# Attention with a memory, then a mixture of experts: one pass for the last keys' two parts, and a new table for the planner

## The chip, the cores and the metric

The kernel runs on one core of a Trainium2 chip. Five engines work side by side, each through its own queue in order: TensorE (PE: matmuls, and PEld, its weight loads), VectorE (DVE), ScalarE (ACT), GpSimd (POOL) and SyncE (SP, which here only issues transfers). The metric is the time of one execution in microseconds (us).

## The reference

Four batches of 8 heads, 576 tokens each, 64 numbers per head. Each head's output mixes causal softmax attention with a read of a stored memory matrix. The heads of a token are laid side by side as a row of 512; a gate then sends each of the 2304 rows to one of 8 experts, two matrix products with a ReLU between.

```python
scores = scale * np.matmul(q, k.transpose(0, 1, 3, 2))
scores = np.where(causal, -1000000000.0, scores)
a = np.exp(scores - scores.max(-1, keepdims=True))
local = np.matmul(a / (a.sum(-1, keepdims=True) + 1e-09), v)
mem_out = np.einsum('bhsd,bhde->bhse', q_p, M_prev) / mem_norm
attn = g * mem_out + (1 - g) * local
logits = x @ w_gate + modality_bias[modality_id]     # x: attn as 2304 x 512
out[mask] = gate_w[mask, None] * (np.maximum(x[mask] @ w1[e], 0.0) @ w2[e])
```

## The kernel before

**Precision.** Most matrix products take a high part (a rounded copy, fp32r) and a low part (the rest) of an operand, and add products of both. ACT makes the high part from PSUM, DVE subtracts it and leaves the low one.

**A head** (32 of them, two to a pair) goes through stages: `scores` (L657, 12 matmuls; DVE masks them and takes row minima, L669; ACT makes the exponentials, L675), `ptrans` (L684, 15 transposes, which ACT and DVE turn into `pth` and `ptl`, the high and low probabilities with keys on the partitions, L701 and L703), and `av` (L715 and L720: values times `pth`, then values times `ptl`, into two PSUM tiles). 576 keys are five blocks, the fifth of 64 keys only. In that block `pth` and `ptl` still have 128 partitions; the value tile `vhl` holds zeros in the lower 64 rows. Per pair come `prep_q`, `prep_k`, `prep_v`, `memory` and `combine`, and SP's transfers: natural-layout loads (L512, L515, L516) and copies that stack high and low parts (L568, L569).

**A batch** ends with `gate` (rows to DRAM by SP, L808 and L809, and the logits), `route` (expert of each token: small DVE steps, two groups of tiny matmuls, five scatters of token numbers by POOL into three tables, L920) and `rank` (which expert is largest, DVE L932 to L945). After the first batch the weights of the largest expert are streamed in (`load_w`: SP L978, ACT high part L985, DVE or POOL low part L989).

**Expert groups.** A group u is `fetch` (SP reads token numbers, L1009; DVE merges them, L999 and L1000; POOL gathers rows, L1016) and `slot`: transposes L1042, ACT and DVE parts L1050 and L1052, 8 tiles of 12 matmuls each (L1064; ACT L1073, DVE L1075), then per 128 tokens 24 matmuls (L1086) and a store (ACT L1093, POOL L1024). Groups 0 to 2 (one per early batch, 256 tokens) are planned into the attention; group 3 is the first that needs the tables of the last batch. `swap` frees the attention's memory for the second expert.

**Order.** Nothing is issued as written. `Plan` collects operations with an engine, an estimated duration and a priority, and plays them forward: of the operations that could start within `WINDOW[engine]` ns of the earliest, it takes the one of least priority. A priority is a step number plus an offset from `EARLIER`, by stage and engine. The result is a fixed order on each engine; on the chip an instruction waits for its inputs, and all behind it on its engine wait too.

```python
o.prio = at + self.EARLIER.get((stage, eng), 0.0)
lim = first[0] + self.WINDOW[e]
```

## Time and profile before

| what | us |
|---|---|
| median of three runs (lowest, highest) | 553.35 (551.58, 555.19) |
| the profiled execution | 550.81 |
| its span, first to last instruction | 549.1 |
| PE busy in the span | 497.9 |
| DVE, ACT, POOL busy | 330.5, 329.0, 251.9 |

A busy engine is one with an instruction on record; matmul records overlap, so a matmul's rate is read from the distance of two starts, not from its length. A bracket at a row's end is idle time just before the instruction, with what ended it. The granted clock of TensorE has two levels here, 1.00 (2.4 GHz) and 0.50 (1.2 GHz).

### The profile page before, as it was taken

To read this page: it belongs to the slowest core of one execution; us is meant where nothing else is said; L and a number is where in the kernel's file an instruction comes from. 1 tells how busy PE (TensorE), PEld (TensorE's weight loads), DVE (VectorE), ACT (ScalarE), POOL (GpSimd) and SP (SyncE) were. 2 spreads that over 40 slices of the span, in tenths; PEclk is the share of its full clock that TensorE was granted. 3 is DMA by queue.
4 is the path that set the end of the run, shared out by engine and by line. 5 is a ranking of instruction groups with operands and counts; after the bars stand their busy time and mean duration, and the time that the engine had idled before them with its cause. 6 is when DMAs were issued, how large, how long until landed. Compare 5 with 4: busy or idle time off the path is not lost. (4 is left out here: it accounts for less than half of the span.)

```text
span 549.1 us, 10861 instructions
## 1 busy us (share of the span) xinstructions
PE 497.9 (91%) x3420; PEld 445.1 (81%) x3420; DVE 330.5 (60%) x1066; ACT 329.0 (60%) x923; POOL 251.9 (46%) x257
## 2 busy tenths in 40 slices
PE   8898899987899889979898999769999999999992
PEld 8787888875787778869897898769897987989891
DVE  3788788897798988988878336653315512313010
ACT  4798898986999979979298244333325513222110
POOL 8462984656788768865761062350030004010100
PEclk9799899999899989989899999979999999999997
DMA  5888887988777997953740025474036203000100
GB/s 96 189 206 169 206 201 182 231 189 154 192 176 198 238 189 191 220 164 95 180 110 3 20 61 180 78 233 146 18 96 182 83 19 88 29 19 21 40 0 36
DMA packets 97101, 70.43 MB, mean 128 GB/s; under 512 B 73936, under 2 KB 74320, under 8 KB 97042
## 3 DMA queue, kind: packets, MB, share of 16 engines
q1 hardware_dynamic: 93330, 59.99, 45.2%
q0 software_dynamic: 3712, 9.72, 5.8%
q8 instruction: 28, 0.46, 0.4%
q14 instruction: 31, 0.25, 0.2%
HBM read 32.36 MB, written 10.16 MB: 77 GB/s over the span
## 5 line engine op out<-in xcount | busy, mean ns | idle before, releaser
L675 ACT ACTIVATE P<-P,nm 128x576 f32<-128x576 f32 (+4 forms) x160 | 88.5, 558 | 9.1 <-DVE nm L669 6.0
L1024 POOL DMA_INDIRECT out_dram<-osb,ids x19 | 18.9, 997 | 156.0 <-ACT osb L1093 115.3
L1064 PE MATMUL pa<-xh,w1h 128*128 128x256 f32 (+2 forms) x288 | 84.4, 293 | 2.6 <-ACT xh L1050 2.6
L1064 PE MATMUL pa<-xl,w1h 128*128 128x256 f32 (+2 forms) x288 | 83.4, 290 | 0.5 <-DVE xl L1052 0.3
L1064 PE MATMUL pa<-xh,w1l 128*128 128x256 f32 (+2 forms) x288 | 83.1, 288 | 0.0
L1075 DVE SCALAR_TENSOR_TENSOR hlo<-pa,hh 128x256 fp32r<-128x256 f32 (+1 forms) x72 | 29.8, 416 | 69.8 <-ACT hh L1073 69.7
L703 DVE TENSOR_TENSOR ptl<-pa,pth 128x512 fp32r<-128x512 f32 (+1 forms) x128 | 65.6, 564 | 3.0 <-ACT pth L701 2.4
L1073 ACT ACTIVATE hh<-pa 128x256 fp32r<-128x256 f32 (+1 forms) x80 | 29.0, 367 | 61.1 <-PE pa L1064 54.2
L669 DVE CUSTOM_DVE_ANT_0 P<-pa,maskw 128x320 f32<-128x320 f32 (+3 forms) x160 | 62.2, 427 | 4.2 <-PE pa L657 3.5
L684 PE MATMUL pa<-ident,P 128*128 128x128 f32 x320 | 57.6, 285 | 4.0 <-ACT P L675 3.7
L657 PE MATMUL pa<-ks,qs 128*128 128x192 f32 (+3 forms) x186 | 55.5, 329 | 5.9 <-ACT avt L735 2.9
L1086 PE MATMUL pa<-w2h,hh 128*128 128x512 f32 (+1 forms) x152 | 60.4, 397 | 0.0
L701 ACT ACTIVATE pth<-pa 128x512 fp32r<-128x512 f32 (+1 forms) x128 | 57.0, 511 | 5.0 <-PE pa L684 4.4
L1086 PE MATMUL pa<-w2l,hh 128*128 128x512 f32 (+1 forms) x152 | 59.6, 392 | 0.0
L1064 PEld LDWEIGHTS pa<-xh,w1h 128*128 128x128 f32 x288 | 55.6, 193 | 3.4 <-ACT xh L1050 2.9
L1064 PEld LDWEIGHTS pa<-xl,w1h 128*128 128x128 f32 x288 | 55.6, 193 | 1.2 <-DVE xl L1052 0.9
L1086 PE MATMUL pa<-w2h,hlo 128*128 128x512 f32 (+1 forms) x144 | 56.5, 392 | 0.0
L1064 PEld LDWEIGHTS pa<-xh,w1l 128*128 128x128 f32 x288 | 55.5, 193 | 0.0
L1093 ACT ACTIVATE osb<-pa,ids 128x512 f32<-128x512 f32 (+1 forms) x19 | 13.1, 687 | 68.4 <-PE pa L1086 63.1
L657 PE MATMUL pa<-kls,qs 128*128 128x192 f32 (+3 forms) x186 | 49.2, 295 | 0.4 <-DMA kls<-kl 0.4
L684 PEld LDWEIGHTS pa<-ident,P 128*128 128x128 f32 x320 | 40.4, 147 | 6.3 <-ACT P L675 6.0
L684 PE MATMUL pa<-swp,P 128*128 128x128 f32 x160 | 39.5, 287 | 6.1 <-DVE kl L617 2.5
(234 smaller groups left out, 1198.9 us busy)
## 6 DMA issues: line engine op xcount, KB each, us to landing
ks<-kh SPq DMA_DIRECT2D x62, 144.0 KB, 3.0
kls<-kl SPq DMA_DIRECT2D x62, 144.0 KB, 3.4
raw<-in_moe_w_dram SPq DMA_DIRECT2D x32, 256.0 KB, 3.5
qn<-in_q_dram SPq DMA_DIRECT2D x32, 144.0 KB, 4.3
kn<-in_k_dram SPq DMA_DIRECT2D x32, 144.0 KB, 4.2
qs<-qh SPq DMA_DIRECT2D x31, 144.0 KB, 2.6
qs<-ql SPq DMA_DIRECT2D x31, 144.0 KB, 2.7
vn<-in_v_dram SPq DMA_DIRECT2D x32, 128.0 KB, 3.0
```

Source lines behind the costliest of these rows:

```text
L657: nc.tensor.matmul(t.ap[0:m, o:o + z - x], lhsT=l[:, QS[j]:QE[j]], rhs=r[:, x:z], start=(i == 0), stop=(i == len(terms) - 1))
L669: nc.vector.tensor_tensor_reduce(out=pj[:, x:z], in0=t.ap[0:m, o:o + z - x], in1=mk, scale=-1.0, scalar=nm if x else 3.0e38, op0=ALU.add, ...
L675: g.op("ACT", act_ns(w, False, 2), lambda pj=pj, nm=nm, den=den, w=w: nc.scalar.activation(out=pj[:, 0:w], in_=pj[:, 0:w], func=AF.Exp, sc ...
L684: nc.tensor.transpose(t[:, o:o + P], prow[c % NPB][j][:, kb * P:(kb + 1) * P], swp if j == kb else ident)
L701: g.op("ACT", act_ns(n), lambda t=t, o=o, n=n: nc.scalar.activation(out=hi[:, o:o + n], in_=t.ap[:, 0:n], func=AF.Copy), r=[t], w=[("ph_", ...
L703: g.op("DVE", dve_ns(n), lambda t=t, o=o, n=n: nc.vector.tensor_tensor(out=lo[:, o:o + n], in0=t.ap[:, 0:n], in1=hi[:, o:o + n].bitcast(F3 ...
L1024: g.op("POOL", 1310, lambda: nc.gpsimd.indirect_dma_start(out=out[:, :], out_offset=bass.IndirectOffsetOnAxis(ap=ids[u % 4][0:m, t, 0:1].b ...
L1064: nc.tensor.matmul(hp.ap[:, 0:n_], lhsT=a[:, c, f * P:(f + 1) * P], rhs=x_[:, c, 0:n_], start=(n == 0), stop=(n == 3 * KC - 1))
L1073: g.op("ACT", act_ns(z - a), lambda f=f, hp=hp, i=i, a=a, z=z: nc.scalar.activation(out=hh[i][:, f, 0:z - a], in_=hp.ap[:, a:z], func=AF.R ...
L1075: g.op("DVE", dve_ns(z - a), lambda f=f, hp=hp, i=i, a=a, z=z: nc.vector.scalar_tensor_tensor(out=hlo[i][:, f, 0:z - a], in0=hp.ap[:, a:z] ...
L1086: nc.tensor.matmul(op.ap[0:m], lhsT=a[:, f, ts], rhs=w_[:, f], start=(y == 0 and n == 0), stop=(y == 3 and n == 5))
L1093: g.op("ACT", act_ns(512, True, 1), lambda t=t, op=op, oi=oi: nc.scalar.activation(out=osb[oi][0:m], in_=op.ap[0:m], func=AF.Copy, scale=i ...
```

## The change

1. In the fifth key block, `ptrans` writes the low probabilities of its 64 keys to the lower 64 partitions of `pth`. `prep_v` fills the lower 64 rows of the value block with the same 64 keys, for which SP loads them a second time. One matmul then covers both parts, and the one on `ptl` is dropped: one of 64 columns per head. The high pass waits for that low part, too.
2. Planned durations: four DVE steps of routing get longer ones (`rank` 1000 to 2700 ns), and the second `av` pass 111 ns less.
3. The last five steps (suffix 9) and each early group (ea, eb, ec, fetches fa, fb, fc) get stage names, so offsets, of their own; the whole table and the windows are new.

```diff
-    Plan.WINDOW = dict(zip(("PE", "ACT", "DVE", "POOL", "SP"), (0, 80, 85, 135, 75)))
+    Plan.WINDOW = dict(zip(("PE", "ACT", "DVE", "POOL", "SP"), (5, 115, 65, 125, 90)))
...
-        "w": (0, 1380.25, 0, 286.25, -1110),
+        "w": (0, 2398.75, 0, -26, -1377.5),
...
-            nc.sync.dma_start(out=t[0:64, 4], in_=s2[:, 512:576, :].rearrange("h p d -> p h d"))
+            for j in range(2):
+                nc.sync.dma_start(out=t[64 * j:64 * j + 64, 4], in_=s2[:, 512:576, :].rearrange("h p d -> p h d"))
...
-        for rows, c0, c1 in ((P, 0, 4), (64, 4, 5)):
+        for rows, c0, c1 in ((P, 0, 4), (P, 4, 5)):
...
+            m, low = (64, hi[64:P]) if part == "D" else (P, lo)
...
-            for kb in range(NB):
+            for kb in range(NB if first else NB - 1):
...
+                 [("pl_", 0, "D")] * part, w=[t], alloc=t, prio=prio, act=0.88)
+            g.op("PE", du - 111 * part, lambda part=part: e(ptl[0], False, part), r=vk + [("pl_", 0, x) for x in ky if x != "D"],
...
-        g.op("DVE", 1150, e0, w=["l0", "l1", "pr", "eb"], r=["basec", "modf", "iote", "tid"], prio=prio)
+        g.op("DVE", 1700, e0, w=["l0", "l1", "pr", "eb"], r=["basec", "modf", "iote", "tid"], prio=prio)
...
-        g.op("DVE", 600, e7, r=["rex"], w=["sx", "pr"], prio=prio)
+        g.op("DVE", 750, e7, r=["rex"], w=["sx", "pr"], prio=prio)
...
-        g.op("DVE", 1000, e, r=["basec"], w=["nst"] + ([("perm", 0)] if b == 0 else []) +
+        g.op("DVE", 2700, e, r=["basec"], w=["nst"] + ([("perm", 0)] if b == 0 else []) +
...
+        def at(stage):
+            return stage + ("9" if n >= NH - 5 else "")
...
-    for i, ns in enumerate((2200, 1400, 2600, 2600)):
+    for i, ns in enumerate((2800, 1750, 2600, 2600)):
```

The whole order moves; three places matter below. In the rows, line numbers of the changed kernel are 10 to 12 higher than before (L1042 is L1054, L1064 is L1076, L1086 is L1098).

On PE, after the last batch's routing: `xg20` holds the rows of group 3, `xg0` those of groups 2 and 4, `hh0` and `hlo0` the hidden layer of group 2. Before:

```order
L1064 MATMUL pa6_96<-xl0_110,w1h0_98 128x256
L1064 MATMUL pa6_96<-xh0_109,w1l0_99 128x256
L1042 MATMUL pa3_93<-ident_64,xg20_4300 128x128 x4
L1042 MATMUL pa2_92<-ident_64,xg20_4300 128x128 x4
L1064 MATMUL pa4_94<-xh0_109,w1h0_98 128x256
L1064 MATMUL pa4_94<-xl0_110,w1h0_98 128x256
```

And now:

```order
L1098 MATMUL pa5_95<-w2h0_100,hh0_111 128x512
L1098 MATMUL pa5_95<-w2l0_101,hh0_111 128x512
L1098 MATMUL pa5_95<-w2h0_100,hlo0_112 128x512
L1054 MATMUL pa7_97<-ident_64,xg20_4290 128x128 x4
L1054 MATMUL pa0_90<-ident_64,xg20_4290 128x128 x4
L1098 MATMUL pa6_96<-w2h0_100,hh0_111 128x512
```

Group 3's transposes stood after seven of the eight first-layer tiles of group 2. Now all eight tiles and 36 second-layer matmuls of group 2 stand ahead of them, and the transposes of group 2 itself have moved ahead of the last routing.

On ACT, in the same stretch: `hh0` is the hidden layer of group 2, eight tiles in turn, and `w2h1` the second expert's weights. Before:

```order
L1073 ACTIVATE hh0_111<-pa5_95 128x256
L1073 ACTIVATE hh0_111<-pa1_91 128x256
L985 ACTIVATE w1h1_4292<-raw3_4307 128x512
L985 ACTIVATE w2h1_4294<-raw0_4304 128x512
L1073 ACTIVATE hh0_111<-pa7_97 128x256
```

And now:

```order
L1085 ACTIVATE hh0_111<-pa5_95 128x256
L1085 ACTIVATE hh0_111<-pa7_97 128x256
L997 ACTIVATE w2h1_4284<-raw0_4294 128x512
L1085 ACTIVATE hh0_111<-pa0_90 128x256
L1085 ACTIVATE hh0_111<-pa4_94 128x256
```

Tiles 5 and 6 of group 2 still stand behind a weight conversion. On SP, that weight's load stands right behind the reads of group 3's token numbers.

On DVE, at the third batch's `rank` (its last rows are `rk` to `perm1`), with `ot1` a part of a head's output. Before:

```order
L943 TENSOR_TENSOR rk_123<-rk_123,basec_75 128x8
L944 MAX top_116<-rk_123 128x8
L945 MAX_INDEX perm1_118<-top_116,rk_123 128x8
L740 TENSOR_TENSOR ot1_175<-pa2_92,avt0_173 64x448
L1075 SCALAR_TENSOR_TENSOR hlo0_112<-pa0_90,hh0_111 128x256
```

And now:

```order
L955 TENSOR_TENSOR rk_123<-rk_123,basec_75 128x8
L956 MAX top_116<-rk_123 128x8
L957 MAX_INDEX perm1_118<-top_116,rk_123 128x8
L606 SCALAR_TENSOR_TENSOR ql0_145<-pa4_94,qh0_144 128x288
L606 SCALAR_TENSOR_TENSOR ql0_145<-pa7_97,qh0_144 128x288
```

The output `ot1` no longer stands directly behind `rank`; two heads' scores, 24 matmuls on PE, now stand ahead of the `combine` that reads it, and DVE takes those scores in behind `rank`. On ACT, at the first weights of the first batch, one conversion instead of two now stands in a row, some ten rows later in the order.

## Rows read from the trace of the kernel before

**Rows 1.** The page: busy us, share of the span, instructions
```profile
PE 497.9 (91%) x3420; PEld 445.1 (81%) x3420; DVE 330.5 (60%) x1066; ACT 329.0 (60%) x923; POOL 251.9 (46%) x257
```
**Rows 2.** Busy time by stretch: us, each engine, PEclk, DMA share, GB/s
```profile
0.00:260.00 260.00, 230.90 (x1708) 205.54 (x1709) 213.93 (x727) 225.84 (x671) 180.45 (x192) 0.96 0.78 184
260.00:345.00 85.00, 81.25 (x580) 74.31 (x579) 54.98 (x198) 44.35 (x125) 38.10 (x34) 0.98 0.36 94
345.00:369.00 24.00, 16.34 (x116) 15.30 (x115) 14.90 (x40) 8.72 (x19) 10.42 (x10) 0.86 0.56 140
369.00:540.00 171.00, 169.43 (x1022) 150.00 (x1020) 46.70 (x104) 50.09 (x109) 22.26 (x23) 1.00 0.20 65
```
**Rows 3.** Timeline of PE (start, us): five second-half value passes; two transposes
```profile
62.59 0.91 PE L720 MATMUL pa<-ptl,vhl 128*128 128x448 f32 x5
63.34 0.34 PE L657 MATMUL pa<-ks,qs 128*128 128x192 f32 x1
...
70.59 0.27 PE L684 MATMUL pa<-swp,P 128*128 128x128 f32 x1
70.70 0.27 PE L684 MATMUL pa<-ident,P 128*128 128x128 f32 x1
```
**Rows 4.** Timelines of SP, ACT and PE: the first weights, first batch
```profile
129.28 0.92 SPq L978 DMA_DIRECT2D xg<-in_moe_w_dram  x2
...
135.23 1.40 ACT L985 ACTIVATE w1h<-xg 128x512 fp32r<-128x512 f32 x2 [4.59 <-DMA xg<-in_moe_w_dram]
...
137.26 0.38 PE L657 MATMUL pa<-ks,qs 128*128 128x256 f32 x1 [2.90 <-ACT avt L735]
```
**Rows 5.** Timelines of PE, DVE and POOL at the third batch's rank
```profile
266.40 0.28 PE L1064 MATMUL pa<-xh,w1l 128*128 128x256 f32 x1
266.52 0.27 PE L794 MATMUL pa<-ident,ot 128*128 128x128 f32 x1
269.07 1.07 PE L794 MATMUL pa<-ident,ot 128*128 128x128 f32 x4 [2.27 <-DVE ot L740]
...
265.74 2.15 DVE L943 TENSOR_TENSOR rk<-rk,basec 128x8 f32<-128x8 f32 x1
267.92 0.17 DVE L944 MAX8 top<-rk 128x8 f32<-128x8 f32 x1
...
266.45 1.40 POOL L603 TENSOR_TENSOR ph<-ph,ex 128x576 f32<-128x576 f32 x1
```
**Rows 6.** Busy time in three stretches of low clock, columns as in rows 2
```profile
139.50:142.90 3.40, 3.29 (x16) 2.95 (x15) 0.58 (x3) 3.35 (x13) 2.95 (x3) 0.50 0.95 233
269.20:272.60 3.40, 3.40 (x18) 3.40 (x19) 2.65 (x8) 0.82 (x2) 2.53 (x3) 0.50 0.25 70
361.40:368.10 6.70, 4.51 (x20) 4.25 (x21) 4.55 (x11) 3.22 (x8) 4.49 (x5) 0.50 0.83 225
```
**Rows 7.** Timeline of PE from the last routing to group 3
```profile
332.77 0.48 PE L863 MATMUL pa<-ident,lgs 16*128 16x16 f32 x5
...
344.82 1.04 PE L1042 MATMUL pa<-ident,xg 128*128 128x128 f32 x8
348.48 0.39 PE L1064 MATMUL pa<-xh,w1h 128*128 128x256 f32 x1 [2.62 <-ACT xh L1050]
...
362.13 0.45 PE L1042 MATMUL pa<-ident,xg 128*128 128x128 f32 x1 [3.25 <-issue]
364.03 1.75 PE L1042 MATMUL pa<-ident,xg 128*128 128x128 f32 x7 [1.46 <-DMA xg<-x_dram,ids]
```
**Rows 8.** Timelines of SP and ACT in the same stretch
```profile
353.92 3.29 SPq L1009 DMA_DIRECT2D idr<-tbl  x6
357.48 0.97 SPq L978 DMA_DIRECT2D raw<-in_moe_w_dram  x2
...
347.25 0.69 ACT L1093 ACTIVATE osb<-pa,ids 128x512 f32<-128x512 f32 x1 [4.33 <-DMA out_dram<-osb,ids]
...
360.19 0.63 ACT L985 ACTIVATE w1h<-raw 128x512 fp32r<-128x512 f32 x1 [4.96 <-DMA raw<-in_moe_w_dram]
```
**Rows 9.** SP's issue of the fifth value block: ns, min/median/max
```profile
L516 SPq DMA_DIRECT2D vn<-in_v_dram x16: 611/656/2398, 4.5 to 250.4; - x16
```

More of the change, by code (lines that the diff above doesn't have):

```diff
@@ L383 @@
     pth = ring(ap_, "pth", 1, [P, 1600], F32R)
-    ptl = ring(ap_, "ptl", 1, [P, 1600], F32R)
+    ptl = ring(ap_, "ptl", 1, [P, 1536], F32R)
     avt = ring(ap_, "avt", 1, [P, S])
@@ L700, in ptrans @@
                  alloc=t, prio=prio)
[L701 to L704 removed]
+            m, low = (64, hi[64:P]) if part == "D" else (P, lo)
+            g.op("ACT", act_ns(n), lambda t=t, o=o, n=n, m=m: nc.scalar.activation(
+                out=hi[0:m, o:o + n], in_=t.ap[0:m, 0:n], func=AF.Copy), r=[t], w=[("ph_", 0, part)], prio=prio)
+            g.op("DVE", dve_ns(n), lambda t=t, o=o, n=n, m=m, low=low: nc.vector.tensor_tensor(
+                out=low[:, o:o + n], in0=t.ap[0:m, 0:n], in1=hi[0:m, o:o + n].bitcast(F32), op=ALU.subtract),
                  r=[t, ("ph_", 0, part)], w=[("pl_", 0, part)], prio=prio)
@@ L720, in e @@
                     nc.tensor.matmul(tb.ap[:, q0 - P:S - P], lhsT=vt[:, kb, hh], rhs=src[:, s0:s0 + S - q0],
-                                     start=(first and kb == 0), stop=(not first and kb == NB - 1))
+                                     start=(first and kb == 0), stop=(not first and kb == NB - 2))
         vk = [(x, p % 2, c) for x in ("vh", "vl") for c in (0, 4)]
         for part, (t, du, ky) in enumerate(((ta, 155, "AB"), (tb, 780, "ABCD"))):
-            g.op("PE", du, lambda part=part: e(pth[0], True, part), r=vk + [("ph_", 0, x) for x in ky], w=[t], alloc=t,
-                 prio=prio, act=0.88)
-            g.op("PE", du, lambda part=part: e(ptl[0], False, part), r=vk + [("pl_", 0, x) for x in ky], w=[t], prio=prio,
-                 act=0.88)
+            g.op("PE", du, lambda part=part: e(pth[0], True, part), r=vk + [("ph_", 0, x) for x in ky] +
+                 [("pl_", 0, "D")] * part, w=[t], alloc=t, prio=prio, act=0.88)
+            g.op("PE", du - 111 * part, lambda part=part: e(ptl[0], False, part), r=vk + [("pl_", 0, x) for x in ky if x != "D"],
+                 w=[t], prio=prio, act=0.88)
         o_, a_ = ot[p % 2][64 * hh:64 * hh + 64], avt[0][64 * hh:64 * hh + 64]
@@ L1234 @@
     mctx = ExitStack()
-    attn = [o for o in g.ops if o.stage not in ("r", "w", "f", "e")]
+    attn = [o for o in g.ops if o.stage[:1] not in set("rwfe")]
     def swap():
```

95 lines of the change are left out of this document (50 added, 45 removed).

## Prediction

> **What bounds the kernel now.** First the page's busy times: PE is on record for 91% of the span, no other engine for more than 60% [rows 1]. Then the busy time by stretch [rows 2]. From 369 us to the end PE is busy for 169.4 of 171.0 us: nothing but fewer matmuls shortens that. From 260 to 345 us it is busy for 81.3 of 85. The loss is in two places: 29.1 us idle in the first 260 us, where DVE (82%) and ACT (87%) are nearly as full and the transfer engines stand at 0.78, and 7.7 us idle in only 24 us from 345 to 369, where the tables of the last batch are waited for. Last come the timelines of PE at its longest idle times, and of the engine that ended each [rows 4, 5, 7, 8]. The reader should see there that a wait is paid twice: behind each of three of them stands a stretch at the lower clock, 0.50, in which PE is busy but half as fast [rows 6]. With PE on record for 3.29 and 3.40 of 3.4 us, such a stretch costs about 1.7 us, and the one at 361 us about half of 4.51, 2.2 us.
>
> **The dropped matmul.** 32 matmuls of 64 columns go, all before the last group of attention ends. Five such passes, 1472 columns, take 63.34 - 62.59 = 0.75 us from start to start [rows 3]. By columns the fifth is 64/1472 of it, 0.03 us, or 1.0 us for 32. Were it bound by its weight load, it would cost what a 128-column transpose does, 70.70 - 70.59 = 0.11 us [rows 3], or 3.5 us. I take the middle, 0.07 us or 2.2 us, and count 2.0, as PE is on record for 89% of that stretch (230.9 of 260, rows 2), so that a little falls into idle time [rows 2]. The new wait of the high pass, for a low part of 64 columns, has the matmul behind it as cover: the matmuls of four other blocks stand ahead of the one that reads it. ACT's and DVE's instructions on that block keep their columns, and POOL's take 128 rows instead of 64 at the same columns, so I price them at nothing; if a row more cost anything, POOL has 80 us of idle time in the first 260 [rows 2].
>
> **The second load of 64 keys.** 16 more transfers, on SP ahead of the copies that `scores` waits for. Each holds SP for 0.66 us (median), once for 2.4 [rows 9], so 10.5 us of SP's time in all over some 250 us. I charge nothing: the longest PE waits above end on ACT, DVE and the routing chain, not on a copy. The cover is the lead that the copies have; where it is gone, the price is up to 0.66 us a pair, 10.5 us (a rival below). A rule of the Trainium skill speaks against this edit: DMA: Bandwidth & Descriptors, Specifications, asks for 512 bytes or more for the full rate, and these rows are of 256 bytes; no row here separates that cost.
>
> **The first batch's weights.** ACT stood 4.59 us before the first conversion, for a load issued by SP at 129.28, and behind it were the copies that free PSUM for `scores`: PE idle 2.90 us [rows 4], then a low-clock stretch of about 1.7 [rows 6]. `rank`, which the load waits for, was planned at 1000 ns, so ACT came too early. With 2700 the conversion stands later and alone. Its load still lands 135.23 - 129.28 = 6 us after its issue, so I expect a shorter wait, not none: 1.5 us gained, between 0 (ACT waits as before) and 4.6 (both losses gone).
>
> **The third batch's rank.** PE waited 2.27 us for a head's output that stood behind `rank` on DVE, and 1.7 us went at the low clock behind it [rows 5, 6]. That output has moved away. But now 24 score matmuls stand on PE at that place; they fill all eight PSUM banks, and DVE empties them only after `rank`. So what is late next is DVE on these scores. I take 1.5 us gained, between -1 and 4. Within `rank` one step of 8 columns took 2.15 us, where the next took 0.17; it ended at 267.89, and POOL's add from 266.45 to 267.85 [rows 5]. The Trainium skill has a rule on this (SBUF — State Buffer, Who interferes with whom): a VectorE instruction with two SBUF inputs and a GpSimd one that reads SBUF exclude each other for a whole instruction. This trace's two ends, 0.04 us apart, agree. By the rule no planned constant fits `rank`, and a POOL instruction at the wrong moment gives this term nothing instead of 1.5.
>
> **From the last routing to group 3.** Time runs from the routing's transposes at 332.77 [rows 7]. Before, PE idled 2.62 us for group 2's parts (they stood on ACT behind an output copy that waited 4.33 us, rows 8), 3.25 and 1.46 for group 3's rows, and lost 2.2 at the low clock: 9.5 us [rows 6, 7, 8]. Now: a second-layer matmul costs (344.82 - 332.77)/48 = 0.25 us [rows 7], a first-layer one 0.12 [rows 5]. Group 2's parts are made before the routing, so the 2.62 goes. The second routing matmuls come 12 first-layer matmuls later, 1.4 us. Before, the token numbers were read at 353.92, 21.2 us after the start [rows 8]; now at 22.6, and group 3's rows are all there at 364.03 - 332.77 + 1.4 = 32.7. PE's work ahead of their transposes is 78 second-layer matmuls, 19.5, and 96 first-layer ones, 11.5, with small ones 31.3: nearly enough. But in it stands a new wait. ACT makes tiles 5 and 6 of group 2 behind a weight conversion, and that weight's load stands on SP behind three reads of token numbers (3.29/6 = 0.55 each): issued at 24.3, landed about 2.7 later (357.48 to 360.19, rows 8), and with 0.63 for the conversion and some 1.3 for two tiles on ACT and DVE the matmuls can go on at about 29. PE is there after 54 second-layer and 96 first-layer matmuls, 25.3. Wait 3.7, low clock about 2, 0.5 for what follows: 6 us against 9.5. I take 3.5, between -1 (both waits add) and 9.5 (ACT is free in time).
>
> **The sum.** 2.0 + 1.5 + 1.5 + 3.5 = 8.5 us. The rest of the order is new as well, and I can't follow all of it; I charge 2.3, the size of one gap as at 269 us [rows 5]. Net 6.2: 550.8 - 6.2 = 544.6 for an execution like the profiled one, which lies 2.5 below the median; 553.3 - 6.2 = 547 as a median.
>
> **The rivals.** *It does not come: the waits move.* ACT still stands before its first conversion, DVE is late on the 24 scores, and the wait in group 2 is as long as the ones it replaces. Then 2.0 minus 2.3 is left, or a bit more: 549.5 to 555. For it: in each of these places the trace shows an engine held by a transfer, and the new order has the same kind of instruction there. Against it: three separate waits would all have to be replaced. *Better: the last part closes.* ACT reaches tiles 5 and 6 before the weight is due, no low clock follows: 6 us more from that part, 536 to 543. For it: 31.3 us of work against 32.7 needed. Against it: the order on ACT above. *Slower: SP sets the pace of attention.* Each pair's copies come 0.66 us later; once their lead is used up, the 16 pairs lose up to 10.5 us. The gains shrink too: with half of the 8.5 left and the 2.3 charged it is 553.3 + 10.5 - 4.3 + 2.3 = 562, with all of them 558. It decides where PE's waits name the copied keys or queries. For it: transfers stand at 0.78 of all 16 engines [rows 2], and single loads took 2.4 us to issue [rows 9]. Against it: none of the long waits ends on a copy.
>
> **How the numbers follow.** Forecast, 543 to 549.5: 0.45. Waits move, 549.5 to 556: 0.28. Closes, 536 to 543: 0.15. Slower, above 556: 0.12. A measurement of this kernel tells about 1% from no change, 5.5 us: faster lies below 547.8, slower above 558.9. Faster: 0.15 and most of the forecast, 0.50. Slower: most of the last case, 0.11. The same: 0.39. For 8 in 10 the range runs from 539.5, which leaves out part of the better case, to 555, which leaves out the slower one and a little of the second. The forecast's own range is 543 to 549.5.
>
> **What would show it.** PE has 3388 matmuls, 32 fewer, and the value pass on `ptl` four per head. PE's wait named by ACT's copies at the first weights is below 2.9 us. Behind the third `rank` no wait of 2.27 for a head's output, perhaps one for scores. After the last routing no wait for group 2's parts, one of about 3.7 us within its second layer named by ACT or DVE, then little before group 3's transposes. The prediction is wrong if the idle time of the first 260 us grows past 29 us, if PE waits for copies, or if the last stretch idles more than 7.7 us.

## The result, and the profile after

The changed kernel takes 556.27 us (median of 20 runs, 552.57 to 559.99), the kernel before 550.74 us (median of 20, 545.06 to 558.24): the ratio is **1.0126, 95% interval 1.0095 to 1.0156**. That ratio is one of means of fast runs, which leaves out the six slowest of the kernel before (over 553.2 us) and none of the changed one; over all 20 the ratio of the means is 1.0090 and that of the medians 1.0100. So it is slower, by 5 to 7 us. The forecast was 547.0 against a median of 553.35 for the kernel before, a ratio of 0.9885, with a range up to 555.0. The profiled execution spans 554.8 us where the one before spanned 549.1.

The page's busy times, as in [rows 1]: PE has its 32 matmuls fewer, and is busy for as long as before.

```profile
PE 497.5 (90%) x3388; PEld 443.2 (80%) x3388; DVE 338.0 (61%) x1066; ACT 328.4 (59%) x923; POOL 252.2 (45%) x255
```

Busy time by stretch, with the columns of [rows 2] (us; PE, PEld, DVE, ACT, POOL; PEclk; DMA share; GB/s). The third stretch is cut longer than in [rows 2], since the work it holds came later.

```profile
0.00:260.00 260.00, 223.67 (x1638) 198.77 (x1638) 213.72 (x707) 219.46 (x655) 178.74 (x189) 0.95 0.77 184
260.00:345.00 85.00, 79.38 (x575) 72.85 (x575) 55.75 (x177) 48.09 (x137) 34.64 (x30) 0.96 0.33 82
345.00:376.00 31.00, 26.66 (x163) 22.79 (x162) 19.09 (x73) 7.97 (x16) 10.74 (x9) 0.89 0.49 113
376.00:545.00 169.00, 167.82 (x1018) 148.82 (x1017) 49.48 (x111) 52.90 (x116) 27.09 (x27) 1.00 0.24 74
```

PE's idle time in the first 260 us has grown from 29.1 to 36.3 us. In the stretch before group 3, where it was 7.7 us of 24, it is 4.3 of 31. So the gain is where the prediction looked for it, and a larger loss where it did not look. Of the three signs of being wrong that the prediction named, the first came (idle time past 29 us) and the third did not (7.7 us idle in the last stretch); the second, waits for copies, is below.

One place splits the two cleanly: the last matmul of the attention (the gate of the last batch). In both kernels PE has done the same work by then, 180 first-layer and 48 second-layer matmuls of the early groups among it; only 8 transposes more stand ahead of it after. The timeline of PE has it at 331.15 us before and at 341.10 after (start, us, line).

```profile
331.15 0.28 PE L826 MATMUL pa<-ql,wgs 128*16 128x256 f32 x1
```
```profile
341.10 0.28 PE L838 MATMUL pa<-ql,wgs 128*16 128x256 f32 x1
```

PE's last matmul ends at 538.7 before and at 544.1 after. **So the attention became 10.0 us longer, and all behind it 4.6 us shorter (207.6 to 203.0).** About 1 us of both is these 8 transposes [rows 7]. Of the 10.0 us, 9.1 are idle time of PE, 42.0 us where there were 32.9. The first matmul of a head's value pass (heads counted from 0) shows where the 10 us arose:

| value pass of head | 1 | 3 | 10 | 13 | 16 | 19 | 27 | 31 | attention's end |
|---|---|---|---|---|---|---|---|---|---|
| before, us | 29.5 | 45.1 | 107.0 | 130.6 | 160.0 | 187.6 | 256.2 | 305.4 | 331.1 |
| after, us | 26.8 | 50.2 | 110.0 | 139.9 | 166.0 | 194.1 | 267.4 | 311.9 | 341.1 |
| difference | -2.7 | +5.1 | +3.0 | +9.3 | +6.0 | +6.5 | +11.2 | +6.5 | +10.0 |

It comes in two steps: 8 us between heads 1 and 3, and 6 between 10 and 13, where PE idles 3.0 us more than before and has 6.8 us of half clock (1.2 GHz) that were not there. At head 13 PE has done the same work but for a few matmuls (885 against 894, 13 of them dropped), and is 9.3 us late. What looks like a third step, some 5 us between 19 and 27, is work that moved: PE has 392 matmuls between heads 20 and 27 where it had 362, and 292 instead of 348 from there to head 31. PE's waits by what they waited for (us in total, times, longest) name several causes. First the rows of the changed kernel, then those of before.

```profile
PE pa L694 <- ACT P L685: 7.1, 6, 1.9
PE pa L727 <- DVE ptl L715: 6.8, 8, 3.8
PE pa L1098 <- ACT hh L1085: 4.3, 2, 2.4
PE pa L667 <- DMA kls<-kl: 4.1, 4, 1.6
...
PE pa L667 <- DMA qs<-ql: 1.5, 2, 1.3
```
```profile
PE pa L684 <- ACT P L675: 4.2, 6, 1.9
...
PE pa L715 <- DVE ptl L703: 2.4, 7, 1.2
...
PE pa L657 <- DMA kls<-kl: 0.4, 1, 0.4
...
PE pa L657 <- DMA qs<-qh: 0.3, 1, 0.3
```

Waits for copies went from 0.7 to 5.6 us, those of the first value pass for DVE's subtraction from 2.4 to 6.8, those of the transposes for ACT's exponentials from 4.2 to 7.1, and L1098 is the new wait in the tail (all that lies behind the attention) that the prediction had named. Added up over the attention, the waits that DVE ended went from 15.0 to 20.6 us, those that a DMA ended from 1.9 to 7.6. TensorE was granted 1.2 GHz for 34 us of the attention after, 24 before.

### The profile page after: what moved, and what is told of

Read it like the earlier page. It is cut to its first block, busy times and chain, and to the rows that moved or that the text cites. A ratio compares the mean times of both kernels' runs of the same rounds, so it can differ in the third digit from the quotient of the medians.

```text
span 554.8 us, 10817 instructions
## 1 busy us (share of the span) xinstructions
PE 497.5 (90%) x3388; PEld 443.2 (80%) x3388; DVE 338.0 (61%) x1066; ACT 328.4 (59%) x923; POOL 252.2 (45%) x255
## 3 DMA queue, kind: packets, MB, share of 16 engines
q1 hardware_dynamic: 95634, 60.52, 45.1%
## 5 line engine op out<-in xcount | busy, mean ns | idle before, releaser
L685 ACT ACTIVATE P<-P,nm 128x192 f32<-128x192 f32 (+4 forms) x160 | 88.3, 556 | 17.1 <-DVE nm L679 16.9
L1076 PE MATMUL pa<-xh,w1h 128*128 128x256 f32 (+2 forms) x288 | 84.0, 292 | 0.0
L1076 PE MATMUL pa<-xl,w1h 128*128 128x256 f32 (+2 forms) x288 | 82.7, 287 | 0.1
L1076 PE MATMUL pa<-xh,w1l 128*128 128x256 f32 (+2 forms) x288 | 82.5, 286 | 0.0
L1087 DVE SCALAR_TENSOR_TENSOR hlo<-pa,hh 128x256 fp32r<-128x256 f32 (+1 forms) x72 | 29.5, 416 | 68.7 <-ACT hh L1085 63.3
L715 DVE TENSOR_TENSOR ptl<-pa,pth 128x512 fp32r<-128x512 f32 x96 | 61.4, 680 | 14.1 <-ACT pth L713 12.7
L667 PE MATMUL pa<-ks,qs 128*128 128x192 f32 (+3 forms) x186 | 58.2, 337 | 8.6 <-DVE ql L606 1.7
L1098 PE MATMUL pa<-w2h,hh 128*128 128x512 f32 (+1 forms) x152 | 60.8, 400 | 4.3 <-ACT hh L1085 4.3
L1098 PE MATMUL pa<-w2l,hh 128*128 128x512 f32 (+1 forms) x152 | 60.3, 397 | 0.0
L1098 PE MATMUL pa<-w2h,hlo 128*128 128x512 f32 (+1 forms) x144 | 57.3, 398 | 0.0
L1076 PEld LDWEIGHTS pa<-xh,w1h 128*128 128x128 f32 x288 | 54.9, 191 | 0.6
L1076 PEld LDWEIGHTS pa<-xl,w1h 128*128 128x128 f32 x288 | 54.9, 191 | 0.7 <-DVE xl L1064 0.3
L667 PE MATMUL pa<-kls,qs 128*128 128x192 f32 (+3 forms) x186 | 51.3, 304 | 4.1 <-DMA kls<-kl 4.1
L1076 PEld LDWEIGHTS pa<-xh,w1l 128*128 128x128 f32 x288 | 54.9, 191 | 0.0
L667 PEld LDWEIGHTS pa<-ks,qs 128*128 128x128 f32 (+1 forms) x186 | 35.1, 189 | 14.5 <-DVE ptl L715 3.3
```

Source lines behind the costliest of these rows:

```text
L667: nc.tensor.matmul(t.ap[0:m, o:o + z - x], lhsT=l[:, QS[j]:QE[j]], rhs=r[:, x:z], start=(i == 0), stop=(i == len(terms) - 1))
L685: g.op("ACT", act_ns(w, False, 2), lambda pj=pj, nm=nm, den=den, w=w: nc.scalar.activation(out=pj[:, 0:w], in_=pj[:, 0:w], func=AF.Exp, sc ...
L715: g.op("DVE", dve_ns(n), lambda t=t, o=o, n=n, m=m, low=low: nc.vector.tensor_tensor(out=low[:, o:o + n], in0=t.ap[0:m, 0:n], in1=hi[0:m, ...
L1076: nc.tensor.matmul(hp.ap[:, 0:n_], lhsT=a[:, c, f * P:(f + 1) * P], rhs=x_[:, c, 0:n_], start=(n == 0), stop=(n == 3 * KC - 1))
L1087: g.op("DVE", dve_ns(z - a), lambda f=f, hp=hp, i=i, a=a, z=z: nc.vector.scalar_tensor_tensor(out=hlo[i][:, f, 0:z - a], in0=hp.ap[:, a:z] ...
L1098: nc.tensor.matmul(op.ap[0:m], lhsT=a[:, f, ts], rhs=w_[:, f], start=(y == 0 and n == 0), stop=(y == 3 and n == 5))
```

## The experiments

Three things changed at once: the merged pass with its second load, the planned durations, and the table of offsets. The planner answers each edit with another order, so most runs here fix the order. All 2749 planned steps have the same numbers in both kernels, and in a run "in the order of before" or "of the changed kernel" a list of these numbers takes the place of the planner's choice (*old_pass_in_new_order* needs none: with its numbers unchanged the planner comes to the changed kernel's order by itself):

```diff
+    ORDER = (
+        ...
+    )
...
-        while left:
-            ...
+        for i in self.ORDER:
+            o = self.ops[i]
```

Each ratio stands against runs of the kernel before on the same chip. The last columns are read from the profiled execution: the start of the attention's last matmul, and from there to the end of PE's last one. In *traced_durations_only* 108 matmuls of the expert groups moved ahead of that point, so its two numbers don't compare with the others.

| run | ratio | 95% interval | attention ends, us | behind it, us |
|---|---|---|---|---|
| kernel before | 1 | | 331.1 | 207.6 |
| changed kernel | 1.0126 | 1.0095 to 1.0156 | 341.1 | 203.0 |
| merge_in_old_order | 1.0150 | 1.0109 to 1.0190 | 336.5 | 207.6 |
| old_pass_in_new_order | 1.0145 | 1.0103 to 1.0187 | 343.5 | 201.3 |
| old_attention_new_tail | 1.0008 | 0.9971 to 1.0044 | 337.8 | 203.7 |
| extra_load_only | 1.0105 | 1.0062 to 1.0149 | 333.4 | 207.7 |
| one_issue_twice_the_bytes | 0.9989 | 0.9944 to 1.0033 | 329.5 | 209.6 |
| second_issue_few_bytes | 1.0069 | 1.0028 to 1.0111 | 335.1 | 205.2 |
| copy_not_load_old_order | 0.9974 | 0.9931 to 1.0017 | 329.9 | 208.2 |
| copy_not_load_new_tail | 0.9880 | 0.9823 to 0.9938 | 331.0 | 203.4 |
| copy_not_load_new_order | 1.0159 | 1.0114 to 1.0203 | 346.7 | 202.2 |
| new_opening_old_pass | 1.0093 | 1.0054 to 1.0131 | 335.9 | 206.1 |
| new_sp_opening_old_pass | 1.0247 | 1.0201 to 1.0293 | 345.3 | 208.1 |
| old_sp_opening_new_rest | 1.0433 | 1.0383 to 1.0483 | 358.3 | 202.1 |
| new_attention_behind_opening | 1.0221 | 1.0172 to 1.0270 | 342.3 | 208.1 |
| routing_behind_subtractions | 1.0081 | 1.0048 to 1.0114 | 342.2 | 202.0 |
| traced_durations_only | 1.0482 | 1.0441 to 1.0523 | 363.0 | 198.3 |
| first_layer_tiles_first | 0.9908 | 0.9878 to 0.9937 | 327.0 | 204.3 |
| tiles_first_on_both | 0.9900 | 0.9864 to 0.9937 | 328.1 | 202.3 |
| copy_new_tail_beside | 0.9863 | 0.9811 to 0.9914 | 326.2 | 203.2 |

### The merge or the order?

*merge_in_old_order*: all of the merge's code, order of before.

> The merged pass, its second load and its smaller tiles, in the order of the kernel before: every engine and the SP queue get their instructions in that order, except that at 10 of the 32 heads the subtraction of the last part is put ahead of the first value pass, which now reads it. Theory 'order' (the attention lost 10.0 us, from its last matmul at 331.1 to 341.1 us, because of where the new table put things): 2.0 us fewer matmuls and nothing against them, so about 549 us, ratio 0.995 to 1.000. Theory 'merge' (the first pass now waits for a subtraction, and SP issues one load more per pair): the loss of the attention shows here, 555 to 560 us, ratio 1.008 to 1.018.

*old_pass_in_new_order*: the code of the two passes back in the changed kernel, order as changed.

> The two separate passes and the single load of before, in the order of the changed kernel. Theory 'order': as slow as the changed kernel plus the 2.0 us of the 32 matmuls, about 558 us, ratio 1.012 to 1.018. Theory 'merge': the attention gets its 10 us back and the tail keeps its gain of 4.6, about 549 us, ratio 0.99 to 1.00.

*old_attention_new_tail*: the merge; order of before up to the attention's last step, the changed one behind it (`before` and `changed` are the two lists).

```diff
-    ORDER = before
+    ORDER = before[:2248] + [i for i in changed if i not in before[:2248]]
```

> The merged pass; order of before up to the last attention instruction, order of the changed kernel for all that comes behind it. By the two traces the stretch behind the attention took 207.6 us before and 203.0 after. Theory 'order': 549 less 4, about 545 us, ratio 0.985 to 0.995, faster than both kernels. Theory 'merge': 552 to 556 us, ratio 1.002 to 1.010. A third outcome, ratio as that of the merged pass in the old order: the gain of the tail came from what the attention left behind in the changed kernel, not from the order of the tail.

Neither theory alone holds. The merge costs 1.5% in the old order, the new order 1.45% with the old pass, and both together 1.26%: the two do not add. The tail is the clear part. With the attention's order kept and only the tail's changed, the ratio falls from 1.0150 to 1.0008, and the stretch behind the attention from 207.6 to 203.7 us: the gain belongs to the tail's own order, whatever the attention did.

The last columns show the attention as well, over more than one execution: five profiles have its new order (changed kernel, old_pass_in_new_order, copy_not_load_new_order, routing_behind_subtractions, and new_attention_behind_opening from head 6 on) and end it at 341.1 to 346.7 us, with the load and without, with the merge and without; seven have its old order and no issue more on SP, and end it at 326.2 to 331.1. The waits that DVE ended add up to 19.9 to 24.0 us of the attention in the five, and to 14.5 to 18.8 in those with the old order.

### What in the merge costs: a load, its issue, or its bytes?

*extra_load_only* and *second_issue_few_bytes* add a second DMA per pair to the kernel before, of 64 rows and of one; *one_issue_twice_the_bytes* widens the one that is there (in 15 of the 16 pairs):

```diff
             nc.sync.dma_start(out=t[0:64, 4], in_=s2[:, 512:576, :].rearrange("h p d -> p h d"))
+            nc.sync.dma_start(out=t[64:P, 4], in_=s2[:, 512:576, :].rearrange("h p d -> p h d"))
```
```diff
+            nc.sync.dma_start(out=t[64:65, 4], in_=s2[:, 512:513, :].rearrange("h p d -> p h d"))
```
```diff
-            nc.sync.dma_start(out=t[0:64, 4], in_=s2[:, 512:576, :].rearrange("h p d -> p h d"))
...
+                nc.sync.dma_start(out=t[:, 4], in_=bass.AP(tensor=x4.tensor, offset=x4.offset,
+                                                           ap=[[x4.ap[0][0], P]] + list(x4.ap[1:])))
...
```

> The kernel before with nothing but a second load of the last 64 keys per pair of heads, into rows that nothing reads: what the load costs SP and the DMA queue, by itself. As the prediction priced it (hidden by the lead of the copies): 550 to 551 us, ratio 0.998 to 1.003. If SP sets the pace of the attention (16 loads by 0.66 us = 10.5 us): ratio up to 1.019.

> The kernel before, its load of the last 64 keys widened from 64 to 128 rows (15 of 16 pairs; nothing reads the rows added): the packets of the second load, but no instruction more on SP. Theory 'issue' (the 5 us of the second load by itself, ratio 1.0105, are SP's 0.66 us per issue, which delay all copies behind it): 549 to 551 us, ratio 0.997 to 1.003. Theory 'packets' (128 more packets of 256 B per pair hold up the copies on the DMA engines): about 554 us, ratio 1.007 to 1.013.

> The kernel before with a second issue per pair that moves one key of each head (2 packets of 256 B in place of 128). Theory 'issue': about 554 us, ratio 1.007 to 1.013. Theory 'packets': 549 to 551 us, ratio 0.997 to 1.003.

The load by itself costs 1.05%, 5.8 us. The bytes without the issue cost nothing that can be measured (0.9989), the issue almost without bytes 0.69%, 3.8 us. So what is paid for is mostly the issue, SP's time. One thing blurs the comparison: the widened issue held SP for 0.50 us (median) where the narrow one took 0.66, some 2 us less in all, which may hide a small price of the bytes; and the intervals of the two runs with an issue more overlap. PE's waits on transfers say the same; first *extra_load_only*, then *second_issue_few_bytes*, then *one_issue_twice_the_bytes*:

```profile
PE pa L658 <- DMA kls<-kl: 2.2, 4, 0.8
PE pa L658 <- DMA qs<-ql: 2.1, 1, 2.1
PE pa L685 <- DMA qs<-qh: 1.9, 1, 1.9
```
```profile
PE pa L658 <- DMA qs<-ql: 3.9, 1, 3.9
PE pa L658 <- DMA kls<-kl: 1.1, 2, 0.8
```
```profile
PE pa L689 <- DMA qs<-qh: 1.9, 1, 1.9
```

PE waits 6.2 and 5.0 us for copied keys and queries where it waits 2.6 with the bytes alone and 0.7 in the kernel before. All its idle time in the attention is 38.1 and 38.5 us with the issue, 32.3 with the bytes alone and 32.9 before. Of the 10.5 us that 16 issues of 0.66 us hold SP [rows 9], between a third and somewhat over a half reaches the time.

*copy_not_load_old_order* and *copy_not_load_new_tail* drop the second load. The keys of rows 64 to 127 come from rows 0 to 63 by one GpSimd copy per pair (the loop over blocks goes back to 64 rows for the fifth):

```diff
-            for j in range(2):
-                nc.sync.dma_start(out=t[64 * j:64 * j + 64, 4], in_=s2[:, 512:576, :].rearrange("h p d -> p h d"))
+            nc.sync.dma_start(out=t[0:64, 4], in_=s2[:, 512:576, :].rearrange("h p d -> p h d"))
...
+                if c0 == 4:
+                    nc.gpsimd.tensor_copy(vt[64:P, 4], vt[0:64, 4])
```

> The merged pass in the order of before, without the second load: GpSimd copies the finished keys (high and low half, 64 rows of 256 values) from rows 0 to 63 to rows 64 to 127 behind the subtraction that makes the low half. SP's queue is that of before. If the second load was the whole price of the merge (ratio 1.015 in the old order): 547 to 550 us, ratio 0.995 to 1.002. If the wait of the first value pass for the last part's subtraction costs too: 552 to 555 us, ratio 1.005 to 1.010.

> The same copy, with the order of before up to the last attention instruction and that of the changed kernel behind it. With the second load this mix was at ratio 1.0008, 1.4% under the merge in the old order throughout. If load and tail add up: about 542 to 545 us, ratio 0.985 to 0.992. If the attention's end loses to something else (first pass, half clock): 548 to 551 us, ratio 0.996 to 1.003.

In the old order the merge goes from 1.0150 to 0.9974: with the load its whole price is gone, and the wait of the first pass for the last part's subtraction costs nothing that shows. With the new tail it is 0.9880, **faster than both kernels**, and the same program on another occasion gave 0.9863 (*copy_new_tail_beside*, below).

*copy_not_load_new_order* undoes the load in the changed kernel and keeps its order.

> The changed kernel in its own order, with the copy on GpSimd in place of the second load: one part of the change undone, and nothing else. If the second load costs in the new order what it costs in the old one (1.0105, or 1.015 for the whole merge): ratio about 1.000 to 1.004 against 1.0126. If the new order loses its 10 us in the attention for reasons of its own (the old pass in the new order, without the load, is at 1.0145): ratio 1.007 to 1.013.

At 1.0159, above both expectations, it gains nothing. In the new order the second load is not what the time is lost to; the order is, and it loses as much with the two old passes, without load and without copy (1.0145, the gain of its tail included).

### Where the new order loses

*new_opening_old_pass*, *new_attention_behind_opening*: the kernel before in every instruction, with the new order up to head 5, or from there to the attention's end (the second diff).

```diff
-    ORDER = before
+    ORDER = changed[:491] + [i for i in before if i not in changed[:491]]
```
```diff
+    x = before[:471] + [i for i in changed if i not in before[:471]]
+    ORDER = x up to its last step of the attention, then the others as in before
```

> The kernel before in all its instructions; the order of the changed kernel up to the last value pass of head 5 (about 62 us), the order of before behind it. In the trace of the changed kernel heads 3 to 5 end 5.1, 4.0 and 3.7 us later than before. If the opening's order costs that and nothing later gives it back: ratio 1.005 to 1.009. If a later wait swallows it: 0.998 to 1.002.

> The kernel before in all its instructions; order of before up to the last value pass of head 5, order of the changed kernel from there to the end of the attention, order of before behind it. The opening by itself was at 1.0093; in the trace of the old pass in the new order the attention ends 12.4 us later than before, 4.1 of which head 5 had. If the rest adds up: 8 us, ratio 1.010 to 1.018. If the half-clock stretches and waits of the rest came from the late opening: 1.000 to 1.005.

The opening alone costs 0.93%, 5.1 us, and never gets it back: head 5 comes 3.2 us late, head 27 3.3, the attention's end 4.8. The rest costs more, 2.21% where 1.8 was the most expected, 11.2 us at the attention's end, and it needs no late opening for that: head 5 is 1.8 us early there, head 10 0.8 late, head 13 7.0 and head 27 11.1. The old pass in the new order throughout has head 27 10.9 us late and the attention's end 12.4. So by these profiles most of what the opening loses is covered by what comes behind it, and the step between heads 10 and 13 is there with either opening. By the ratios the two add (0.93% and 2.21%, against 1.45% with a tail that gains 1.4), so how much the opening adds in the end is not settled.

What the opening loses is read from the timelines of SP and PE. First the kernel before:

```profile
24.93 0.98 SPq L568 DMA_DIRECT2D ks<-kh  x1
...
29.22 0.55 SPq L568 DMA_DIRECT2D kls<-kl  x1
...
30.50 1.14 SPq L515 DMA_DIRECT2D vn<-in_v_dram  x2
...
34.31 1.57 SPq L456 DMA_DIRECT2D tbl<-xb  x3
```

then the changed one:

```profile
18.93 1.52 SPq L465 DMA_DIRECT2D tbl<-xb  x3
...
25.83 1.00 SPq L524 DMA_DIRECT2D vn<-in_v_dram  x2
...
28.68 0.51 SPq L578 DMA_DIRECT2D ks<-kh  x1
...
33.72 0.58 SPq L578 DMA_DIRECT2D kls<-kl  x1
...
33.40 0.33 PE L667 MATMUL pa<-kls,qs 128*128 128x192 f32 x1 [1.26 <-DMA kls<-kl]
...
38.07 0.50 PE L667 MATMUL pa<-kls,qs 128*128 128x192 f32 x1 [1.55 <-DMA kls<-kl]
```

The copies of the second pair's keys start 3.75 us later (28.68 against 24.93) and their last part 4.50 (33.72 against 29.22): the zero fills of the tables (`tbl`) and the value loads (`vn`), which stood behind them, now stand ahead. PE waits for the copies twice, and its clock is at 0.50 from 34.8 to 41.6 us.

*new_sp_opening_old_pass* and *old_sp_opening_new_rest* exchange only the first 31 steps of SP's queue.

```diff
-    SP's steps in ORDER = sp_before
+    SP's steps in ORDER = sp_changed[:31] + sp_before[31:]
```

> The kernel before with only the first 31 steps of SP's own queue in the changed kernel's order (zero fills of the tables, loads of queries and values ahead of the copies of the second pair's keys); PE, ACT, DVE and GpSimd as before. If SP's order makes the loss of the opening (the changed kernel waits 1.26 and 1.55 us for key copies at 33.4 and 38.1 us, half clock behind it): ratio 1.004 to 1.009, as the whole opening. If not: 0.998 to 1.002.

> The changed kernel with only the first 31 steps of SP's queue in the order of before: the reverse. If SP's order makes the loss of the opening: 4 us less than the changed kernel, ratio 1.003 to 1.008. If not: 1.010 to 1.015.

Both came out far worse (1.0247 and 1.0433), each way round. That does not test what it was meant to test: PE, ACT and DVE kept an order that was planned with the other queue, and in the first of the two PE stood 3.96 and 4.55 us at key transposes for loads that were now issued late. They show only that this part of SP's queue can't be exchanged alone. That SP's order makes the loss of the opening is read from the timelines, and no run shows it.

*routing_behind_subtractions*: the changed kernel with three routing steps of DVE moved, nothing else. The list of VectorE's queue before and after the edit, by step numbers:

```diff
-739 740 987 990 993 996
+987 990 993 996 739 740
...
-1338 1480 1483 1486
+1480 1483 1486 1338
```

> The changed kernel with three of VectorE's routing steps moved in its queue and nothing else: the first batch's last two (sums and destinations) behind the four subtractions of the next head's probabilities, the second batch's one-hot step behind three. In the changed kernel's trace PE waits there 1.81 and 1.03 us (129.0 and 130.4) and 3.79 us (194.1), each with 6.8 us of half clock behind it. Theory 'VectorE': these waits go, 6.6 us and up to 3.4 us of half clock each, ratio 0.993 to 1.005 where the changed kernel has 1.0126. Rival: the routing, later now, holds up PE at its own matmuls or the table writes instead, ratio 1.010 to 1.018.

The ratio is 1.0081, between the two expectations, where the changed kernel has 1.0126; the intervals overlap, so a gain is not shown. In its profile the attention ends at 342.2 us, no earlier, though that execution took 3.9 us more than the run's median. The wait of 3.79 us at 194 us went, head 19 came 3 us sooner than in the changed kernel, and smaller ones took its place by head 20. The longest in PE's timeline are 1.06 us for a load of keys at 190.57 and 1.69 us for DVE at 195.69.

*traced_durations_only*: the planned durations of the routing in the kernel before (two of the five numbers shown), its table kept.

```diff
-        g.op("DVE", 1150, e0, w=["l0", "l1", "pr", "eb"], r=["basec", "modf", "iote", "tid"], prio=prio)
+        g.op("DVE", 1700, e0, w=["l0", "l1", "pr", "eb"], r=["basec", "modf", "iote", "tid"], prio=prio)
...
-        g.op("DVE", 1000, e, r=["basec"], w=["nst"] + ([("perm", 0)] if b == 0 else []) +
+        g.op("DVE", 2700, e, r=["basec"], w=["nst"] + ([("perm", 0)] if b == 0 else []) +
```

> The kernel before with the planned durations of the routing steps alone raised to the changed kernel's (1150 to 1700, 600 to 750, 1000 to 2700, 2200 and 1400 to 2800 and 1750 ns), its table of offsets kept. If truer durations help by themselves (the third batch's rank, 2.27 us and 3.4 us of half clock behind it): ratio 0.992 to 0.998. If the old table was fitted to the old durations, and a plan with others is any plan: 1.003 to 1.015.

1.0482 is well outside both expectations. The truer numbers move other steps too: PE stands 13.8 us before group 3's transposes and 9.8 us for subtractions of the value pass (8 waits, the longest 5.9).

The old table was good only together with the old numbers. The new table with the old durations was not run, so what the durations and the table bring each is not told apart here.

### Can the rest of the wait before group 3 be ordered away?

In the new tail PE still waits in group 2's second layer. *first_layer_tiles_first* takes four tiles of ACT (`hh`) ahead of two weight conversions, *tiles_first_on_both* also the last two `hlo` of DVE ahead of a merge of token lists. By steps:

```diff
-2342 1915 1918 2345 1921 1924 2348 1927 1930
+2342 1915 1918 1921 1924 1927 1930 2345 2348
```
```diff
-1922 1925 2372 2340 1928 1931
+1922 1925 1928 1931 2372 2340
```

> The copy in place of the load, old attention, new tail (0.988), and in ScalarE's queue the last four first-layer tiles of group 2 ahead of the two weight conversions that waited for their loads. There PE waits 1.23 and 2.65 us for these tiles (358.0 and 362.4), with half clock behind it. If ScalarE's order is the cause of that wait, as the prediction named it: 3.9 us and 1.7 us for the half clock less, ratio 0.975 to 0.983. If the loads set the time there anyway: 0.985 to 0.992.

> As first_layer_tiles_first (0.9908), and in VectorE's queue the last two low halves of group 2's first layer ahead of the merge of the group's token lists and of a weight subtraction, behind which they waited: there the wait of 3.9 us had come back as 2.28 us (356.98). If that was all that took its place: 2.3 us less than first_layer_tiles_first in a like state of the clock, ratio 0.980 to 0.988. If the next transposes of tokens wait instead (0.65, 0.46 and 1.43 us at 363 to 368 so far): 0.986 to 0.992.

> The kernel of copy_not_load_new_tail (0.988) on the same chip and against the same runs of before as tiles_first_on_both, so that the two can be compared directly. Theory 'queue order in the tail pays': this one is slower than tiles_first_on_both by 2 to 5 us. Theory 'the waits only move': the two are within 1.5 us. Ratio 0.984 to 0.992 either way.

The wait goes where the edit sends it, and the time stays: 0.9908, 0.9900, and without either edit 0.9880 and 0.9863. On one chip and against the same runs of before, both edits together have a median 2 us above that of none, and the intervals overlap. PE's timeline shows it moving, in *copy_new_tail_beside*, then in *first_layer_tiles_first*, then in *tiles_first_on_both*:

```profile
353.82 0.50 PE L1189 MATMUL pa<-w2h,hh 128*128 128x512 f32 x1 [1.76 <-ACT hh L1176]
...
357.78 0.50 PE L1189 MATMUL pa<-w2h,hh 128*128 128x512 f32 x1 [2.30 <-ACT w2h L1088]
```
```profile
356.98 0.50 PE L1189 MATMUL pa<-w2h,hlo 128*128 128x512 f32 x1 [2.28 <-DVE hlo L1178]
```
```profile
361.75 0.30 PE L1145 MATMUL pa<-ident,xg 128*128 128x128 f32 x1 [0.84 <-issue]
...
364.06 0.98 PE L1145 MATMUL pa<-ident,xg 128*128 128x128 f32 x7 [2.01 <-DMA xg<-x_dram,ids]
...
367.82 0.47 PE L1145 MATMUL pa<-ident,xg 96*128 96x96 f32 x3 [0.94 <-DMA xg<-x_dram,ids]
```

4.1 us for `hh` (the second row names the weight conversion that stood ahead of it on ACT), then 2.3 for `hlo`, then 3.8 before group 3's transposes. As these rows read, what ends last is the arrival of group 3's rows, behind the read of the token numbers and their gather; as long as that chain keeps its start, PE only chooses where to stand.

## Why the prediction was wrong, by its own steps

**The rest of the order, charged at 2.3 us: the step that failed.** The prediction followed the order at three places and priced everything else at "the size of one gap". The old pass in the new order ends the attention 12.4 us later than before, with 9.4 us more idle time of PE and none of the merge. The opening alone makes 4.8, the new order from head 6 on alone 11.2. That rest was not traced to one wait. Its one step that stands out, heads 10 to 13, holds the first batch's routing on DVE, and waits that DVE ended are what all profiles with the new order have more of; but the one attempt to take waits away there (three routing steps moved) brought others in their place, and head 13 came no earlier (140.2 against 139.9). Which of its steps the order loses this by is left open.

**The second load, priced at nothing: wrong in its cover.** "The longest PE waits above end on ACT, DVE and the routing chain, not on a copy" was true of the trace of before, and said nothing of how much lead the copies had. It was too small: in the trace of before SP's issues, added up, fill 0.83 of the first 60 us and 0.82 of the next 60, and 5.8 of the possible 10.5 us came through by the load alone, 3.8 by its issue alone. The Trainium skill (DMA: Bandwidth & Descriptors, Specifications) gives 512 bytes as the least size of a transfer for the full rate; by bytes no cost shows here, twice the 256-byte rows in one issue is at 0.9989. In the changed kernel's own order the load's removal gains nothing, so this error did not decide the result.

**The slower rival** named the sign to look for, PE waits on copied keys or queries, and it came, 5.6 us where there were 0.7. But its mechanism was the load, and with the old single load the new order has the wait too (3.1 us on `kls`). The sign was right, and the load was not its cause. Its size, 558 to 562, is 4.7 to 8.7 us above the 553.3 it was worked out from; the changed kernel is 5 to 7 above its own kernel before, so the size came as well, by luck. Where the load is the mechanism, in merge_in_old_order, it is 8.1 (557.25 against 549.12).

**The dropped matmul, 2.0 us (1.0 to 3.5).** Without the load and in the old order the merge is at 0.9974, 1.4 us less, interval 3.8 less to 0.9 more: in agreement, and too small for the time to show. PE's busy time shows it, in one pair of profiles: in the same order, with the same 34.1 us of half clock, it is 299.2 us up to the attention's end in the changed kernel and 301.3 with the two old passes, 2.1 less.

**The first batch's weights, 1.5 us (0 to 4.6): the wait went altogether.** ACT stands 0.15 us before the first conversion where it stood 4.59 [rows 4], and no PE wait of 2.90 follows.

```profile
141.72 0.63 ACT L997 ACTIVATE w1h<-xg 128x512 fp32r<-128x512 f32 x1 [0.15 <-DMA xg<-in_moe_w_dram]
```

But the half clock is granted all the same, from 130.4 us and for twice as long as at 139.5 before, behind waits on DVE's routing steps. PE's timeline, and the stretch with the columns of [rows 6]:

```profile
129.04 0.33 PE L694 MATMUL pa<-swp,P 128*128 128x128 f32 x1 [1.81 <-DVE l L916]
...
130.39 0.43 PE L727 MATMUL pa<-pth,vhl 128*128 128x128 f32 x1 [1.03 <-DVE ptl L715]
```
```profile
130.40:137.20 6.80, 6.72 (x29) 6.23 (x30) 4.53 (x15) 4.62 (x14) 3.74 (x4) 0.50 0.49 82
```

With PE on record for all of that stretch it costs 3.4 us. The gain at the named place was real, and the loss moved to its neighbour.

**The third batch's rank, 1.5 us (-1 to 4): below its lower end.** The wait of 2.27 us for a head's output [rows 5] is gone. Scores wait in its place, as "perhaps one for scores" had it, 3.2 us in three pieces:

```profile
275.05 0.33 PE L667 MATMUL pa<-ks,qs 128*128 128x192 f32 x1 [1.26 <-DMA qs<-ql]
...
276.35 0.47 PE L667 MATMUL pa<-ks,qs 128*128 128x448 f32 x1 [0.54 <-DVE basec L929]
...
278.70 0.53 PE L667 MATMUL pa<-ks,qs 128*128 128x192 f32 x1 [1.39 <-DVE ql L606]
```

Behind the first two stands twice the half clock of before; the stretch, with the columns of [rows 6]:

```profile
277.20:284.00 6.80, 5.41 (x23) 4.87 (x23) 5.70 (x31) 2.62 (x9) 5.53 (x5) 0.50 0.31 65
```

Counted as the prediction counted, 2.27 and 1.7 us became 3.2 and 2.7: 1.9 us lost. It was right that DVE on the scores is late next (two of the three waits name DVE), and priced that as the smaller loss.

**From the last routing to group 3, 3.5 us (-1 to 9.5): right, and its mechanism for half of what is left.** No wait for group 2's parts is left, and none before group 3's transposes. Two waits of 1.94 and 2.40 us stand within group 2's second layer, behind weight conversions on ACT (one of 3.7 was forecast; timelines of PE, ACT and SP). The second is the one forecast: its weight's load was issued at 368.59, behind three reads of token numbers on SP. The first was not: its conversion started at 367.02, for a load issued before 356.8, ahead of these reads, and why that load landed so late is open:

```profile
367.97 0.50 PE L1098 MATMUL pa<-w2h,hh 128*128 128x512 f32 x1 [1.94 <-ACT hh L1085]
...
372.19 0.79 PE L1098 MATMUL pa<-w2h,hh 128*128 128x512 f32 x1 [2.40 <-ACT hh L1085]
...
367.02 0.63 ACT L997 ACTIVATE w1h<-raw 128x512 fp32r<-128x512 f32 x1 [5.40 <-DMA raw<-in_moe_w_dram]
...
371.24 0.63 ACT L997 ACTIVATE w2h<-raw 128x512 fp32r<-128x512 f32 x1 [3.04 <-DMA raw<-in_moe_w_dram]
...
345.01 11.74 SPq L990 DMA_DIRECT2D raw<-in_moe_w_dram  x7
366.83 1.50 SPq L1021 DMA_DIRECT2D idr<-tbl  x3
368.59 0.33 SPq L990 DMA_DIRECT2D raw<-in_moe_w_dram  x1
```

All that lies behind the attention took 4.6 us less (3.6 without the transposes that moved ahead of it), 3.9 with the old attention. **The better rival** (the part closes, 6 us more) failed for the reason that the sum itself had worked out, rows due at 32.7 us against 31.3 of work: with both queues of tiles freed PE stood before these rows instead.

**"The waits move"** is what happened, in the attention more than at the three places it was written for. It was held against it that "three separate waits would all have to be replaced". They need not be replaced at their places; a new order of 2749 steps makes new waits anywhere in 330 us.

## What to carry to other kernels

A new order is not the sum of the places that one follows in it: first find where the work of a stage ends, before and after, and price what was not followed by a whole new set of waits of the trace's kind, here 10 us, not by one gap. One more issue on a queue that is busy for four fifths of a stretch can be paid for even when no wait of the present trace names that queue (here in the old order, not in the new), and an on-chip copy by an engine with idle time can take its place. A planner's durations, the order it finds and the work it orders belong together: each of them changed alone was slower here. The good half (the new tail, and the merge with the copy in place of the load) without the rest was worth 1.2 to 1.4%.

## What the runs showed of the hardware

The same small VectorE instruction took five to ten times as long beside GpSimd. `oh<-l` (128x40, L892) took 0.12 us for the first batch and 1.18 for the second; `sx<-sx` (128x5, L924) took 1.27 us for the first and 0.17 for the second. Both long ones ended within 0.03 us of a GpSimd instruction's end (189.44 and 128.66 us). Of the eight such instructions in the changed kernel, the four with a GpSimd instruction beside them took 0.88 to 1.27 us, the four without 0.12 to 0.17. The timelines of DVE and POOL in the changed kernel:

```profile
113.29 0.12 DVE L892 TENSOR_SCALAR oh<-l 128x40 f32<-128x40 f32 x1
...
188.29 1.18 DVE L892 TENSOR_SCALAR oh<-l 128x40 f32<-128x40 f32 x1
...
188.18 1.26 POOL L786 TENSOR_TENSOR mt<-mt,rnm 128x640 f32<-128x640 f32 x1 [1.55 <-DVE rnd L795]
...
127.41 1.25 POOL L786 TENSOR_TENSOR mt<-mt,rnm 128x640 f32<-128x640 f32 x1 [0.35 <-DVE sx L923]
127.42 1.27 DVE L924 TENSOR_SCALAR sx<-sx 128x5 f32<-128x5 f32 x1
```

The prediction had this from a step of `rank` with two inputs in SBUF. These have a single tensor input. The Trainium skill (SBUF — State Buffer, Who interferes with whom) names `tensor_scalar` among the operations that can take both ports and then exclude GpSimd; the rows agree. A planned duration is then right for one of the two cases at most: "traced" durations are those of the order in which they were traced.

Two profiles of one program, copy_not_load_new_tail and copy_new_tail_beside, differ by 5.1 us in span (544.8 and 539.7), and in the mean granted clock (0.970 and 0.982). Up to PE's last matmul the first was granted the half clock for 23.9 us and the second for 13.7: PE was busy 3.9 us longer in the first and idle 1.1 us longer, so the half clock is most of the difference. How much of it is granted varies by several microseconds of time from one execution of a program to the next, and a single profile of this kernel cannot settle a difference of 1%.
